# Cross-attention between tokens and states, then a feed-forward layer with the SERF activation: new orders for the first tenth of the program, and a one-element activation ahead of six activations that wait for two engines

## The chip, the core and the metric

The kernel runs on one core of a Trainium2 chip. The metric is the device time of one execution in microseconds (us). Five engines take part, each with a list of its own that it works through strictly in order: TensorE (PE; its weight loads are shown apart as PEld), VectorE (DVE), ScalarE (ACT), GpSimd (POOL) and SyncE (SP), which here only issues DMA transfers. An instruction that has to wait for another engine stops everything behind it in its own list. All products are in fp32.

## What is computed

```python
scores = scale * np.matmul(x, state.transpose(0, 1, 3, 2))     # x: 8 x 8 x 512 x 64, state: 8 x 8 x 32 x 64
a = softmax over the 32 states;      xread = np.matmul(a, state)
a2 = softmax over the 512 tokens of scale * state @ x^T;  sread = np.matmul(a2, x)
t = concatenate([xread, sread], axis=2)        # reshaped to 4352 x 512 (8 batches x 544 rows)

h = t @ w_in                                   # 512 x 2048
sp = np.maximum(h, 0.0) + np.log1p(np.exp(-np.abs(h)))        # softplus
g = h * erf(sp)
out = g @ w_out                                # 2048 x 512
```

## The kernel before

**Work.** The eight batches are handled one after the other, with 512 token rows each; the 32 state rows of all batches are gathered and handled together further back. The hidden width of 2048 is split into two halves u of 1024. For one batch and one half there is a *unit*: a first product into `h`, Softplus and Erf on ACT, the product with `h` on DVE, a second product with `w_out`. The units after batch 0 use a scheme that needs seven block products instead of eight; that is why DVE forms many sums and differences of blocks (`sums_y`, `sums_a`, `sums_w`, from lines 882, 996 and 1011).

**The first tenth.** Batch 0 and half u = 0 start with nothing loaded, and take another way (`begin0`, from line 382):

- `x` of batch 0 comes in four transfers of two heads each, two issued by ACT and two by SP. PE turns each part (L421), ACT or DVE copies it out of PSUM (`xT`, L164 or L170), and PE forms the scores (L447) in two groups g of four heads.
- For each group: copies of the scores, PE turns them (L453), DVE takes the maximum and subtracts it (L472, L474), ACT takes Exp (L477), DVE sums, inverts and multiplies (L479, L120 and L121, L482), PE turns the result (L457), and a copy makes `aT` (`ta0`, `ta1`).
- Meanwhile `w_in` and `w_out` of the first half arrive in pieces of 1 MB, in three buffers `raw`, and are rewritten by ACT and DVE (`convert`, from line 555: two activations L561 and L563, a shift L565, a sign step L570 or L573, an addition L579) because of a change of number format on the way.
- PE makes `m`, the product of `w_in` and the states (`mixed0`, L608), in parts: hidden blocks 0, 1, and 2 with 3. `first0` (L626) multiplies `m` with `aT`; ACT takes Softplus (L633) and Erf (L638); DVE multiplies (L642); `second0` (L651) multiplies with `w_out`, 32 products of 0.86 us. The first `first0` is the first product that isn't preparation.
- PE also turns the states of all batches (`turn_states`, L674), which come in two halves, `load_states` 0 and 1, four small transfers each (L662).
- Between these, PE runs spare products on the identity matrix (`spare_products`, L115), whose results nobody reads.
- The other direction of batch 0's attention (`later`, from line 490) takes its Exp on ACT (L498), and batch 1's attention (`attend`, from line 697) begins.

**What sets the order.** The kernel records every operation with `op(engine, cost, at, go, reads, writes, table)` into a list. `ORDER` then holds, written out by hand for each engine, the order in which that engine issues its operations; the numbers count the operations of that engine in recording order. `emit` merges the five lists into one program by estimated times, which doesn't alter an engine's own order, and `in_order` ties each instruction to the one before it on its engine. `BY_VECTOR` names copies that DVE makes; those that aren't named there ACT makes.

**Tables of ACT.** Exp, Softplus and Erf each need their own table in ACT. When the function changes, the compiler puts an ACT_TABLE_LOAD directly ahead of the activation. `op` is told of it by `table`. In the built program, an activation that waits for one engine has its load ahead of the wait; for some that wait for two engines, the first of the two waits stands ahead of the load and the second behind it. The program has 53 table loads before.

Two places far behind the first tenth matter too: the Softplus at 224.15 us (`first_product` of a later batch, `soft` at L971), which waits for DVE and PE, and the Softplus at 306.43 us, which waits for DVE and ACT itself. Behind each of them ACT makes copies (L961 and L919 in the one, L1280 in the other) that PE waits for.

Of the kernel before, what the change touches and what calls it, by code (L numbers as in the profile page):

```python
# [17 lines left out]
def kernel(  # L18
# [17 lines left out]
    nc = tc.nc  # L36
# [103 lines left out]
    def op(engine, cost, at, go, reads=(), writes=(), table=None, land=0.0, pipe=0.0):  # L140
# [14 lines left out]
        x0 s00 ta1 i00 i1 o0 o1 i2 i3 o2 o3 z0 z1 m000 m010 m011 m020 m021 u0 u1 m120 m121 tw1 sn10  # L155
        sn11 o9 i11 o11 i13 o13 i14 i15 o15 sn20 sn21 sn40 sn41 sn50 sn51 sn61 sn71""".split())

    def either(name, cost, out, in_, at, reads, writes, by=None, run=None):
# [15 lines left out]
        else:  # L174
# [4 lines left out]
            0 5 1-2 8 3 6 4 15 9 7 13 10 17 12 22 18 16 19 23 20 11 24-25 21 14 26 28 27 29-32 34 33  # L179
            45 70 69 62 53 46 61 54 71 48 55 35 72 37 56 36 38 64 39-40 49 41 47 50 73 57 74 58 60  # L180
            59 76 75 43 42 66 44 77-78 52 51 79-80 82 81 83 63 84 86 85 93 89 88 65 67 90 68 87 102
            91-92 94 97 103 106 95 107 104 108 105 109 118 114-115 110 116 96 111 117 119 99 98
            112-113 122 130 123-124 132-133 125 131 134 137 120 135 121 136 140 139 138 141 126
# [32 lines left out]
            0-1 5 2-3 6 4 13 12 8 7 15 14 9 17 31 16 11 18 10 20 51 19 52 32-34 36 21-22 35 24 37 23  # L216
            26 25 38-39 41 28 27 40 42 30 29 44 43 47 46 45 49 56 50 48 53-54 60 58-59 62 61 55 63
            96 65 64 66 69 67 70 72 68 89 71 90 74 81-82 73 83 75 84 78 77 76 79-80 85-88 57 91 146
            92 97 93 137 94 136 98-100 148 103 95 104 138-141 150 102 143 147 151 144 152 105 149
            153 101 142 154 159 155 161 160 157 156 162 164 158 163 165-168 145 172-173 169 175 174  # L220
            170 110 178 106-107 171 179 111 184 188 108 112 190 109 189 191 180 192 197 181-182 199
            198 200 194 193 195 202 113 201 196 204 185 177 176 211 210 114 183 186 203 214 213 212
            215 205-207 224 117 116 187 226 208 115 227 209 216 225 220 228 217 121 218 120 233 122
            234-235 118-119 236 238 237 229 123 239 241 247 246 221 219 240 231 251 250 232 248 222
            230 124 249 260 242-245 262 223 261 253 252 254 129 126 125 256 263 266 264 269 127 271
            128 272 255 273 268 275 130 270 131 258 132-133 284 283 285 282 135 257 134 276 274 265
            267 277-278 287-288 297 259 279-280 299 290 281 300 293 298 289 291 286 301 306 308
            303-304 309 307 294 302 312 292 311 314 310 313 295 305 315-317 296 322 319 318 320 345
            323 321 325 324 347 330 348 346 326 349 331 350 327-328 354 333 356 351 332 357 353 355
            358-359 361 334 340 352 329 360 335 362-363 341 364 336 365-366 343 342 338 344 337 387  # L230
            372 339 367-368 373 375 374 370 376 382 388 371 369 389-390 383 377 385 393 392 378 391
            395 394 400 396-397 384 379 398 380 402 399 381 403-404 401 407 386 408 415 413 416
            405-406 414 409 418 410-411 420-421 419 412 424 422 427 429 425 423 430 433 431 434 428
            432 426 435-437 440 438 443 442 441 417 439 464 466 465 449 444 467 450 445 470 452 468
            451 446 473 475 447 453 448 471 469 476 474 472 478 477 480 459 479 454 481-482 455 460
            483 488 486 489 462 487 461 484 510 457 485 463 456 511-512 458 513 495 490 514 519 496
            518 491 497 521 492 498 493-494 522 499 520 515 524 517 516 523 526 500 525 527-528 501
            534-535 505 532 503 529 502 533 506 530 507 556 508 558 531 559 509 504 536 560 557 541
            537 542 562 565 544 538 566 539 564 563 567-568 571 543 569 561 570 540 545-546 578-580
            573 581 551 572 574 552 575 602 576 554 553 577 547 604 549 548 605 550 603 555 606 587  # L240
            582 611 588 590 613 610 591 589 583 609 585 608 614 607 584 617 586 619 615 618 597 612
            616 620-621 598 592 626 622 624 627 625 594 599-600 593 648 595 601 623 596 633 650 649
            651-652 634-635 657 654 628-629 655 636 659 630 658 631 660 653 637 656 661 643 663 662
            664 632 644 665-666 646 645 667-668 670 673 638 672 639 647 669 640-641 671 694 642 696
            679 695 674 697-698 680 675 703 700 681 705 676-677 682 678 706 702 699 704 709 707 711
            684 683 689 716 719 701 718 708 710 685 712 717 740 713 690 714-715 691-692 687 741-743
            693 744 686 725 749 688 726 746 720 751 745 750 721 728 722 752 727 723 753 755 729 748
            747 756 724 754 735 757-758 730 759-760 731 761 736 733 732 738 737 734 739 762-763 765
# [1480 lines left out]
```

## Time and profile before

| | |
|---|---|
| median of three runs | 696.99 us (696.93 to 697.43) |
| the profiled execution | 696.16 us |
| its span in the trace | 694.3 us |
| granted TensorE clock | 0.999 |
| PE busy | 686.8 us |
| DVE busy | 581.7 us |
| ACT busy | 480.1 us |
| POOL busy | 85.8 us |

The span goes from the first to the last instruction in the trace; the execution's own time holds 1.86 us more around it. Times in the trace count from the start of the span. "Busy" adds up the instructions of an engine; in a row of the timeline the first number is the start, the second how long the row's instructions took from the first start to the last end, and a bracket at the end tells how long the engine had been idle before, and which engine and instruction ended that. PE rows follow each other with an overlap, because matmuls are pipelined: the distance from start to start is what a row costs.

### The profile page before, as it was taken

To read this page: it belongs to the slowest core of one execution; us is meant where nothing else is said; L and a number is where in the kernel's file an instruction comes from. 1 tells how busy PE (TensorE), PEld (TensorE's weight loads), DVE (VectorE), ACT (ScalarE), POOL (GpSimd) and SP (SyncE) were. 2 spreads that over 40 slices of the span, in tenths; PEclk is the share of its full clock that TensorE was granted. 3 is DMA by queue.
4 is the path that set the end of the run, shared out by engine and by line. 5 is a ranking of instruction groups with operands and counts; after the bars stand their busy time and mean duration, and the time that the engine had idled before them with its cause. 6 is when DMAs were issued, how large, how long until landed. Compare 5 with 4: busy or idle time off the path is not lost.

```text
span 694.3 us, 13176 instructions
## 1 busy us (share of the span) xinstructions
PE 686.8 (99%) x5193; PEld 584.0 (84%) x5193; DVE 581.7 (84%) x899; ACT 480.1 (69%) x850; POOL 85.8 (12%) x93
## 2 busy tenths in 40 slices
PE   9999999999999999999999999999999999999997
PEld 8435678787878788889998879898989898989997
DVE  5999899998989799989945779785969586949897
ACT  6987998988886695747255574848574857477742
POOL 0001000010001110000100000024101331312312
PEclk9999999999999999999999999999999999999999
DMA  9847976977889517425454302436322663721675
GB/s 266 231 141 177 180 233 155 216 199 187 287 171 276 169 49 267 125 84 152 119 157 166 84 1 61 122 42 119 46 69 31 118 89 71 105 31 18 89 138 107
DMA packets 133741, 92.87 MB, mean 134 GB/s; under 512 B 93744, under 2 KB 120752, under 8 KB 133168
## 3 DMA queue, kind: packets, MB, share of 16 engines
q1 hardware_dynamic: 113648, 61.29, 32.3%
q0 software_dynamic: 18800, 29.63, 22.8%
q10 hardware_dynamic: 1232, 1.11, 0.5%
q8 instruction: 41, 0.67, 0.4%
q14 instruction: 20, 0.16, 0.1%
HBM read 50.86 MB, written 41.16 MB: 133 GB/s over the span
## 4 chain that ended last, share of the span: by engine, by line
PE 93%; DVE 4%; ACT 1%; DMA 1%; issue 1%; SPq 0%; DVEq 0%; ACTq 0%
PE o L1270 31%; PE h L949 18%; PE o L1033 16%; PE at L949 7%; PE o L651 4%; PE o L1454 4%; PE h L1405 3%; PE h L850 2%; PE at L850 2%; PE at L626 1%; PE at L1405 1%; DVE ring L1000 1%; PE at L811 1%; PE h L718 1%; DMA x<-in_x_dram 1%; PE o L115 1%
## 5 line engine op out<-in xcount | busy, mean ns | idle before, releaser
L961 ACT COPY ring<-h 128x512 f32<-128x512 f32 x120 | 69.4, 586 | 70.9 <-PE h L949 66.3
L989 DVE TENSOR_TENSOR ring<-ring 128x1024 f32<-128x1024 f32 (+1 forms) x64 | 72.9, 1151 | 24.9 <-ACT ring L986 24.3
L949 PE MATMUL h<-aT,m 128*128 128x256 f32 x360 | 92.0, 380 | 0.0
L971 ACT ACTIVATE ring<-ring 128x512 f32<-128x512 f32 x120 | 72.2, 631 | 10.8 <-DVE ring L967 4.9
L1033 PE MATMUL o<-w_out,ring 128*128 128x256 f32 x320 | 77.1, 381 | 0.0
L1000 DVE TENSOR_TENSOR ring<-ring 128x1024 f32<-128x1024 f32 x60 | 72.6, 1217 | 0.4
L949 PEld LDWEIGHTS h<-aT,m 128*128 128x128 f32 x360 | 65.3, 190 | 8.5 <-issue 1.0
L1033 PEld LDWEIGHTS o<-w_out,ring 128*128 128x128 f32 x320 | 59.9, 190 | 13.1 <-issue 2.5
L1270 PE MATMUL o<-w_out,w_in 128*128 128x128 f32 x512 | 68.7, 275 | 0.0
L1270 PEld LDWEIGHTS o<-w_out,w_in 128*128 128x128 f32 x512 | 64.3, 192 | 1.5
L1270 PE MATMUL o<-w_out,ring 128*128 128x128 f32 x480 | 64.7, 275 | 0.6 <-ACT oo L1280 0.6
L1270 PEld LDWEIGHTS o<-w_out,ring 128*128 128x128 f32 x480 | 60.6, 192 | 3.0 <-ACT oo L1280 1.0
L986 ACT ACTIVATE ring<-ring 128x1024 f32<-128x1024 f32 (+1 forms) x64 | 62.8, 1007 | 0.2
L1033 PE MATMUL o<-raw,ring 128*128 128x256 f32 x240 | 58.9, 380 | 0.0
L1033 PEld LDWEIGHTS o<-raw,ring 128*128 128x128 f32 x240 | 45.1, 190 | 7.1 <-issue 0.8
L1270 PE MATMUL o<-raw,ring 128*128 128x128 f32 x360 | 49.5, 275 | 0.0
L1270 PEld LDWEIGHTS o<-raw,ring 128*128 128x128 f32 x360 | 46.1, 192 | 2.0 <-DVE sc L1285 0.8
L1270 PEld LDWEIGHTS o<-raw,xT 128*128 128x128 f32 x320 | 38.8, 192 | 3.7 <-ACT o L1301 2.5
L1270 PE MATMUL o<-raw,xT 128*128 128x128 f32 x320 | 41.5, 277 | 0.0
L1189 POOL DMA_DIRECT2D out_dram<-oo x16 | 23.0, 1526 | 126.0 <-ACT x L1280 62.3
L949 PE MATMUL h<-sy,sx 128*128 128x256 f32 x120 | 31.4, 385 | 0.8 <-ACT h L919 0.8
L949 PE MATMUL h<-sy,m 128*128 128x256 f32 x120 | 31.1, 382 | 0.0
(269 smaller groups left out, 1398.8 us busy)
## 6 DMA issues: line engine op xcount, KB each, us to landing
x<-in_x_dram SPq DMA_DIRECT2D x30, 256.0 KB, 5.0
xq<-in_x_dram SPq DMA_DIRECT2D x112, 64.0 KB, 2.6
out_dram<-oo SPq DMA_DIRECT2D x10, 512.0 KB, 3.9
raw<-in_moe_w_in_dram SPq DMA_DIRECT2D x8, 512.0 KB, 6.5
raw<-in_moe_w_out_dram SPq DMA_DIRECT2D x4, 1024.0 KB, 6.2
raw<-in_moe_w_in_dram POOLq DMA_DIRECT2D x8, 512.0 KB, 6.5
raw<-in_moe_w_out_dram POOLq DMA_DIRECT2D x8, 512.0 KB, 5.5
kept_a<-aT SPq DMA_DIRECT2D x8, 512.0 KB, 4.5
```

The source lines that it names most:

```text
L651: nc.tensor.matmul(out=bank("o%d" % r), lhsT=gT[g][:, i, P * r:P * r + P], rhs=w_out[:, GF * g + i, :], start=(made_of[r] == 1), stop=(mad ...
L850: nc.tensor.matmul(out=bank(names[k])[Ns * p:Ns * p + Ns, :], lhsT=st[r, b, q], rhs=of_group[2 * u + j][r, :, i, :], start=True, stop=True)
L949: nc.tensor.matmul(out=out_[:, i], lhsT=x_[:, q:q + P], rhs=y_, start=(start and i == 0), stop=(i == 1), skip_group_check=not start)
L961: op(ACT, 0.5, t, lambda: nc.scalar.copy(out_(), view(bank(name))), [name], w)
L971: op(ACT, 0.53, t, lambda: nc.scalar.activation(out=part(splane, k), in_=part(hplane, k), func=ACTF.Softplus), area(hplane, ks=[k], os=[o] ...
L986: op(ACT, 0.085 + 0.875 * share, at + n, lambda s_=s_: nc.scalar.activation(out=s_, in_=s_, func=ACTF.Erf), [], area(splane, ks=[k], os=os ...
L989: op(DVE, 0.065 + 1.075 * share, at + n + 1, lambda s_=s_, h_=h_: tt(s_, s_, h_, op=ALU.mult), area(hplane, ks=[k], os=os), area(splane, k ...
L1000: op(DVE, 1.14, at + k, lambda k=k, x_=x_, y_=y_, how=how: tt(get("h", k), get(*x_), get(*y_), op=how), area(v[x_[0]], ks=[x_[1]]) + area( ...
L1033: nc.tensor.matmul(out=view(name)[:, h], lhsT=lhs[:, i, :], rhs=weight_of[n]()[:, u, i, :], start=(start and h == 0 and i == 0), stop=(h = ...
L1270: nc.tensor.matmul(out=out_[:, Q2 * k:Q2 * k + Q2], lhsT=lhs[:, k, i], rhs=rhs[:, i], start=first, stop=(k == len(ns) - 1 and i == 1), ski ...
L1405: nc.tensor.matmul(out=bank(bk)[:, P * i:P * i + P], lhsT=x_[:, i, k], rhs=y_[:, k], start=(start and i == 0 and k == 0), stop=(i == GF - ...
L1454: nc.tensor.matmul(out=bank("o%d" % bk)[:, E2 * c:E2 * c + E2], lhsT=ring[:, w_[w], plane, k][:, i, :], rhs=weight_of[n]()[:, u, i, :], st ...
```

## The change

Two things are changed in the code.

**1. The first tenth.** `ORDER` is rewritten for the first 79 of 821 operations on PE, 62 of 786 on ACT (64 of 788 after), 90 of 889 on DVE (88 of 887), 25 of 98 on SP and 5 of 84 on POOL; behind that, the order is the same as before on each engine (all numbers on ACT grow by two and those on DVE fall by two, because two more copies are recorded for ACT). `BY_VECTOR` moves these copies:

- from DVE to ACT: the scores `s00`, `aT` half `ta1`, a sign step `i00`, `m000` and `m011`, the copy `tw1`, the state copy `z1`;
- from ACT to DVE: `x3`, the scores `s11`, the sign step `i01`, and `m100` and `m101`.

In the new order the second group of heads goes first: its two parts of `x` are loaded, turned and scored ahead of the first group's, and its half of the first `w_in` piece is loaded and converted ahead of the other half. SP issues the first half of the state loads ahead of the first load for batch 1, and the second 1 MB of `w_out` ahead of the second half of the state loads and of the first loads `xq` for batch 1; further loads `xq` change places with pieces of `w_in` and `w_out`. On ACT the two Exp of the other direction of batch 0 (L498) move from ahead of the first Softplus to between two pairs of Softplus and Erf; on DVE the sums for batch 0 (`sums_y`) move ahead, and on PE the `second0` products change places among each other. On POOL one staged `w_in` load moves ahead, and one staged `w_out` load behind, the store of a piece of batch 0's output.

**2. The one-element activation.** While it goes through the operations, `emit` counts the table loads on ACT; ahead of the operations at loads 2, 4, 9, 11, 26 and 33 it issues an activation of the same function on one element per partition. It reads a constant and writes a tile `spark` that nothing reads. The table load then stands ahead of this activation, and neither waits for another engine. The program has 54 table loads after. Loads 2, 4 and 9 are those of a Softplus of `first0`, load 11 that of Exp in batch 1's attention (L753 before), and loads 26 and 33 are those of the Softplus at 224.15 us and at 306.43 us in the profile before.

```diff
     BY_VECTOR = set("""
-        x0 s00 ta1 i00 i1 o0 o1 i2 i3 o2 o3 z0 z1 m000 m010 m011 m020 m021 u0 u1 m120 m121 tw1 sn10
-        sn11 o9 i11 o11 i13 o13 i14 i15 o15 sn20 sn21 sn40 sn41 sn50 sn51 sn61 sn71""".split())
+        x0 x3 s11 i01 i1 o0 o1 i2 i3 o2 o3 z0 m010 m020 m021 u0 u1 m100 m101 m120 m121 sn10 sn11 o9
+        i11 o11 i13 o13 i14 i15 o15 sn20 sn21 sn40 sn41 sn50 sn51 sn61 sn71""".split())
...
         PE: """
-            0 5 1-2 8 3 6 4 15 9 7 13 10 17 12 22 18 16 19 23 20 11 24-25 21 14 26 28 27 29-32 34 33
-            45 70 69 62 53 46 61 54 71 48 55 35 72 37 56 36 38 64 39-40 49 41 47 50 73 57 74 58 60
-            59 76 75 43 42 66 44 77-78 52 51 79-80 82 81 83 63 84 86 85 93 89 88 65 67 90 68 87 102
+            0 5 3 15 4 1-2 7-8 6 12 17-18 9 13 22 19-21 16 23 25 10-11 24 14 26 28 27 30 29 32 31
+            33-34 46 70 54 53 45 61-62 69 47 56 64 35 72 55 37 36 38 48 71 40 39 41 58 57 50 74 73
+            49 59-60 42-43 75 52 51 44 77-78 76 79 66 82 81 80 83 63 84 86 85 93 89 88 65 67 90 68
...
         ACT: """
-            0-1 5 2-3 6 4 13 12 8 7 15 14 9 17 31 16 11 18 10 20 51 19 52 32-34 36 21-22 35 24 37 23
-            26 25 38-39 41 28 27 40 42 30 29 44 43 47 46 45 49 56 50 48 53-54 60 58-59 62 61 55 63
+            1 0 4 3 2 7 15-16 5-6 12-14 8 10 33 32 17-19 9 34 20 11 35 21 36-37 22 38-39 24 40 23 26
+            25 52 28 27 53 42 41 30 43 29 44-45 47-48 46 50-51 58 49 54 31 55 57 56 61 64 63 62 60
...
         DVE: """
-            0-1 72 2 13-14 73 3 16 15 7 4 8 5 41 6 17 9-10 74 11 42-43 18 12 19-20 22 44-45 21 23 49
-            48 58 47 79 75 24 46 25 28 26 50-51 27 29-30 77 59 80 31 61 32 76 60 34 53 52 82 33 35
-            55 54 117 36-38 65 62 57 66 56 63 40 64 118 81 78 67-70 87-88 83-84 89 85 71 90 86 103
+            1 0 2 72 15 8 16 9 3 13 4 14 71 17 5 10 6 40 7 11-12 18-20 22 77 73 78 42 41 21 43 23 80
+            46 44-45 24-26 28 58 57 47-48 27 29-31 50 49 60 34 32 74 33 76 35 52 51 59 37 75 53-54
+            36 79 115 38 64 61 65 55-56 62-63 116 66-69 85-87 81-82 70 83 88 84 101 89 102 90
...
         SP: """
-            1 0 2 5-6 8 7 9 17 3-4 18 10 23 12 11 13 24 19 14 21 20 15 22 16 25-26 28 27 31 34 29-30
+            1-2 0 6 5 7-9 3 10 4 18 17 11 20 12 14 19 13 15 24 23 16 21-22 25-26 28 27 31 34 29-30
...
         GP: """
-            1 4 6-7 0 5 2 9-10 12-13 8 16 15 11 18 3 14 19 24 17 20-22 25 27 23 26 28-29 31 30 32-34
+            1 4 7 0 6 5 2 9-10 12-13 8 16 15 11 18 3 14 19 24 17 20-22 25 27 23 26 28-29 31 30 32-34
...
     }
+    EARLY = {2, 4, 9, 11, 26, 33}
+    spark = const.tile([P, 1], F32, name="spark")
+
+    def ahead(n):
+        func = {"softplus": ACTF.Softplus, "erf": ACTF.Erf, "exp": ACTF.Exp}[ops[n][5]]
+        go = ops[n][3]
+
+        def after():
+            nc.scalar.activation(out=spark, in_=nc.const_aps.tensor(1.0, [P, 1], F32), func=func)
+            go()
+
+        ops[n] = (*ops[n][:3], after, *ops[n][4:])
+
...
         order = sorted(begin, key=lambda n: (begin[n], n))
+        loaded, loads = None, 0
+        for n in order:
+            table = ops[n][5]
+            if ops[n][0] == ACT and table not in (None, loaded):
+                loaded, loads = table, loads + 1
+                if loads in EARLY:
+                    ahead(n)
         for n in order:
             ops[n][3]()
```

More of the change, by code (lines that the diff above doesn't have):

```diff
@@ L221 @@
[L221 to L240, printed above, removed]
@@ new lines @@
+            374 341 369-370 375 377 376 372 378 384 390 373 371 391-392 385 379 387 395 394 380 393
+            397 396 402 398-399 386 381 400 382 404 401 383 405-406 403 409 388 410 417 415 418
+            407-408 416 411 420 412-413 422-423 421 414 426 424 429 431 427 425 432 435 433 436 430
+            434 428 437-439 442 440 445 444 443 419 441 466 468 467 451 446 469 452 447 472 454 470
+            453 448 475 477 449 455 450 473 471 478 476 474 480 479 482 461 481 456 483-484 457 462
```

115 lines of the change are left out of this document (65 added, 50 removed).

## The prediction

> **What bounds the kernel now.** I read the busy shares and the chain first.
>
> ```profile
> PE 686.8 (99%) x5193; PEld 584.0 (84%) x5193; DVE 581.7 (84%) x899; ACT 480.1 (69%) x850; POOL 85.8 (12%) x93
> PE 93%; DVE 4%; ACT 1%; DMA 1%; issue 1%; SPq 0%; DVEq 0%; ACTq 0%
> ```
>
> PE is busy all the time and carries the chain. So there are only two ways to gain: let PE's real work begin earlier (the spare products in front count as busy, but end nothing), or close the few places where it stands still. The timeline of PE, read to the end for its brackets, has three of these from 60 us on, at 225.91, at 307.65 and a small one further back. The first two are where the change puts its last two small activations. The timeline of all engines around the first, and behind it a row of DVE and the small halt of PE:
>
> ```profile
> 218.12 0.58 ACT L961 COPY ring<-h 128x512 f32<-128x512 f32 x1
> 222.10 0.68 DVE L963 TENSOR_TENSOR ring<-ring,at 128x512 f32<-128x512 f32 x1
> 222.86 1.28 ACT L971 ACT_TABLE_LOAD   x1 [4.16 <-DVE ring L963]
> 223.18 1.89 PE L1033 MATMUL o<-raw,ring 128*128 128x256 f32 x8
> 224.15 0.63 ACT L971 ACTIVATE ring<-ring 128x512 f32<-128x512 f32 x1
> 224.69 0.57 ACT L961 COPY ring<-h 128x512 f32<-128x512 f32 x1
> 225.29 0.57 ACT L919 COPY h<-h 128x512 f32<-128x512 f32 x1
> 225.91 1.13 PE L949 MATMUL h<-sy,sx 128*128 128x256 f32 x4 [0.84 <-ACT h L919]
> 226.88 1.03 PE L949 MATMUL at<-aT,sx 128*128 128x256 f32 x4
> ...
> 232.33 0.69 DVE L963 TENSOR_TENSOR ring<-ring,at 128x512 f32<-128x512 f32 x1 [1.52 <-PE at L949]
> ...
> 539.79 0.71 PE L1270 MATMUL o<-raw,w_in 128*128 128x128 f32 x4 [0.19 <-ACT ot L1280]
> ```
>
> ACT is idle for 4.16 us, then DVE's sum at L963 ends, and only now the table is loaded, 1.28 us; Softplus and two copies follow without a gap, and PE waits for the second. Around the second place:
>
> ```profile
> 302.71 2.35 DVE L1000 TENSOR_TENSOR ring<-ring 128x1024 f32<-128x1024 f32 x2
> 304.01 0.27 ACT L1280 COPY ot<-o 128x128 f32<-128x128 f32 x1
> 305.14 1.28 ACT L971 ACT_TABLE_LOAD   x1 [0.85 <-DVE ring L1000]
> 305.98 1.03 PE L949 MATMUL at<-aT,sx 128*128 128x256 f32 x4
> 306.43 0.63 ACT L971 ACTIVATE ring<-ring 128x512 f32<-128x512 f32 x1
> 307.65 1.61 PE L1270 MATMUL o<-w_out,ring 128*128 128x128 f32 x12 [0.64 <-ACT oo L1280]
> 309.09 1.03 PE L949 MATMUL h<-sy,sx 128*128 128x256 f32 x4
> ```
>
> The same picture with less idle time ahead. For the first tenth, a stretch of busy times (PE, PEld, DVE, ACT and POOL in this order), the timeline of PE, PEld, DVE, ACT and SP, and the transfers by group (the last number is the median from issue to landing):
>
> ```profile
> 30.00:70.00 40.00, 40.00 (x237) 17.82 (x236) 39.29 (x53) 33.02 (x44) 3.36 (x5) 1.00 0.66 168
> 18.11 0.56 ACT L170 COPY aT<-o 128x512 f32<-128x512 f32 x1
> 20.32 1.16 ACT L561 ACTIVATE w_out<-raw 128x1024 f32<-128x1024 f32 x1
> 9.67 0.69 DVE L472 TENSOR_REDUCE m1b<-at 128x16 f32<-128x512 f32 x1 [0.36 <-PE at L453]
> 16.76 0.69 DVE L579 CUSTOM_DVE_ANT_0 w_in<-raw,w_in 128x1024 uint16<-128x1024 uint16 x1 [0.34 <-ACT raw L573]
> 18.58 0.69 DVE L482 TENSOR_TENSOR ring<-ring,z1b 128x512 f32<-128x512 f32 x1
> 19.47 0.60 PE L457 MATMUL o<-ident,ring 128*128 128x128 f32 x4
> 19.91 3.60 PE L626 MATMUL h<-aT,m 128*128 128x512 f32 x8
> 20.19 0.68 DVE L164 COPY aT<-o 128x512 f32<-128x512 f32 x1
> 22.04 1.23 DVE L579 CUSTOM_DVE_ANT_0 w_in<-raw,w_in 128x2048 uint16<-128x2048 uint16 x1
> 23.44 0.66 PE L608 MATMUL at<-w_in,ring 64*32 64x256 f32 x16
> 24.31 0.76 DVE L164 COPY m<-at 128x256 f32<-128x256 f32 x2
> 25.12 0.30 PEld L626 LDWEIGHTS at<-aT,m 128*128 128x128 f32 x2 [0.35 <-DVE m L164]
> 29.26 0.41 DVE L887 TENSOR_TENSOR sy<-aT 128x256 f32<-128x256 f32 x1
> 15.41 3.48 SPq L662 DMA_DIRECT2D st<-in_state_dram  x4
> 20.04 1.29 SPq L587 DMA_DIRECT2D raw<-in_moe_w_out_dram  x1
> raw<-in_moe_w_out_dram SPq DMA_DIRECT2D x4, 1024.0 KB, 6.2
> ```
>
> DVE hardly rests (39.29 of 40 us, and two idle times of a third of a us in the rows before that), so its list decides when PE's real work begins: the second multiply (18.58) ends, PE turns its result (19.47), and the first real product follows at 19.91. From 30 us on PE has no gap in the whole tenth (40.00 of 40.00 us).
>
> **The sum, part by part.**
>
> *The load at 222.86.* With the small activation, load and activation are free to run from 218.70 (218.12 + 0.58). The activation itself isn't in the trace. A Softplus on 512 elements takes 0.63 us and a copy of 128 elements 0.27 us, so I bound one element between 0.1 and 0.3 us and take 0.2. Both end at about 220.2, long before DVE. Softplus starts at 222.86 instead of 224.15, and the copies end 1.29 us earlier; PE could go on at 224.62. Is PE ready then? In a full stream a group starts 0.17 us before the row ahead ends (223.18 + 1.89 = 225.07, so at 224.90). PE would therefore not wait: it gains 225.91 − 224.90 = 1.0, and the first group after the halt, which costs 0.97 (225.91 to 226.88) instead of 0.86, another 0.1. I take **1.1 us**; the bounds are the idle time of 0.84 and the 1.29 by which ACT is earlier.
>
> *The load at 305.14.* It can start at 304.28 (304.01 + 0.27), 0.86 us earlier, but the small activation's 0.2, less some overlap, goes in between: Softplus at about 305.72 instead of 306.43, 0.7 us earlier. DVE's L1000 ends at 305.06 and doesn't delay it. PE could use more: by 0.17 before 307.01 it would be ready at 306.84, 0.81 before 307.65, so ACT stays last there and the gain is **0.7 us** (bounds 0.5 and 0.9).
>
> *What moves behind these places.* After the first, DVE waits for PE again at 232.33, so it has 1.52 us to spare and follows; and from the second on PE is dense, so both gains stay. Nothing else in the unchanged part gets an instruction.
>
> *The added load and the other four small activations.* Two Exp now stand between a Softplus-Erf pair and the next, which adds one load of 1.28 us; four small ones are 0.8 us; the copies that change engine give ACT about 0.5 us net and take as much from DVE. That is 2.6 us more on ACT, which has 40.00 − 33.02 = 7.0 us free between 30 and 70 us. I cost it at nothing. Without that cover each microsecond would reach PE through Softplus and DVE's product.
>
> *When the real products begin.* Up to the second multiply the two DVE lists hold nearly the same instructions: the sign step, the score copy and the `m` copy of the one half for those of the other. The idle times of 0.36 and 0.34 us go; a new one of some 0.6 us comes ahead of the first shift, since its ACT step waits for the first half of `w_in` and that lands no earlier than now. So the multiply, and with it PE's turn, comes by my count of the two lists 0.2 to 0.5 us earlier. On ACT the copy that the first product needs (0.56 us) now stands behind a conversion of the first `w_out` (1.16 us), which waits for a 1 MB transfer; this takes back part. I take **0.3 us**, between −0.5 (the transfer lands late) and +0.7.
>
> *From there to 25.12.* Before, DVE does the two copies of `m`, a copy of `aT` (20.19, 0.68 us) and the shift, sign and addition (ending 23.27) before PE's `mixed0` at 23.44; then comes another sign step, up to 24.31, and the copies of `m` (to 25.07), and PE's weight load waits for these, 0.35 us. After, the `aT` copy and an earlier `m` copy are ACT's, some 0.9 us less on DVE; two sums (0.41 each) come in between, but behind the addition, and DVE starts this stretch some 0.6 us earlier, since its multiply is earlier and one `m` copy stands ahead of it. DVE's copies of `m` then end near 24.3. PE, from 19.6 with four halves of `first0` (3.53, from 19.91 to 23.44) and `mixed0` and the states (1.35, from 23.44 to 25.12 less the wait), gets to its next `first0` at 24.5 and need not wait: **0.3 us**.
>
> *From 25.12 to the common order.* PE is dense before, so other places of its products can gain nothing, and each new wait is a loss. ACT now makes one conversion step (1.16 us) before the Softplus of the second pair, whose Erf and DVE product come close to PE's need; I take **−0.2 us** (bounds 0 and −1).
>
> *The queues.* SP's second half of the states (15.41) and two `xq` loads go behind the second 1 MB of `w_out`, which is issued as soon as its buffer is free. The addition at 16.76 reads that buffer last; the new DVE list has it ahead of two steps more, at about 15.5. By 6.2 us from issue to landing it lands at about 22, and the states, small, behind it at 22.5 to 23.5. PE turns them at about 23.6. I cost this at nothing, with little to spare: the states being late by a microsecond would stop PE for one. The later swaps bring `w_in` and `w_out` pieces no later than now. POOL's three swapped transfers feed conversions that come after 90 us in an unchanged order: nothing.
>
> Sum: 1.1 + 0.7 + 0.3 + 0.3 − 0.2 = 2.2 us. The profiled execution has 696.16 us, so 693.96 after it; the median of the runs, 696.99, is 0.83 higher, which gives 694.8 us.
>
> **A rule against it.** In the trace a load costs ACT its own 1.28 us and no more:
>
> ```profile
> 23.50 1.08 ACT L633 ACTIVATE ring<-h 128x512 f32<-128x512 f32 x2
> 24.61 1.28 ACT L638 ACT_TABLE_LOAD   x1
> 25.90 1.06 ACT L638 ACTIVATE ring<-ring 128x1024 f32<-128x1024 f32 x1
> ```
>
> From load to activation are 1.29 us, and the load starts 0.03 us after the activations ahead of it have ended (23.50 + 1.08). The Trainium skill (ScalarE: Activation LUTs, What ACT_TABLE_LOAD costs) counts a drain of 1380 ns beside the load's 1283 ns, 2.66 us for every switch, and advises to do everything of one table set before changing; by that the second place would lose and the added switch in the first tenth weigh double. The load's length agrees with the trace, the drain doesn't show.
>
> **Rivals.**
>
> *Only the late loads pay.* The first tenth comes out even or slightly worse, because DVE's list is as full as before and the gain at 19.91 goes to the `w_out` conversion or to the second pair's Softplus: 1.8 us less a few tenths, 695.2 to 695.8. For it: each of the three early terms is of the size of my error in it.
>
> *Switches cost more where they follow work.* If a switch cost a second load's length, 1.28 us, as a halt behind it, load and small activation from 304.28 would end near 307.0, later than 306.43: a loss of 0.6. The added switch and halt would eat more of ACT's free time, and I count half a load, 0.6, as a loss; the first place still gains 1.1 and the early part 0.4: 697.0 − 1.1 + 0.6 − 0.4 + 0.6 = 696.7, no change. The rows from 23.50 on speak against it. The rule of the Trainium skill (ScalarE: Activation LUTs) would, with its 1380 ns, make this 0.1 us more per switch.
>
> *The states come late (slower).* If the 1 MB lands only 10 us after its issue, or the small transfers take their turn well after it, PE stands ahead of `turn_states` with everything behind. The loss is the landing time of the states minus 23.6. It eats the forecast from 25.8 on, and makes the kernel slower by 0.2% from 27.2 on; at 28 it would be 699.2. For it: the 6.2 us is a median of four and says nothing of the longest, and SP took 3.48 us to issue these small transfers. Against: it would have to be late by 2.2 us before the forecast is eaten.
>
> *The first tenth gains more.* DVE's list is shorter by about 1.3 us up to the common order. If PE follows it, 693.5.
>
> **How the numbers follow.** The forecast has 0.46, only the late loads 0.22, dearer switches 0.07, late states 0.10, the greater gain 0.15. About 0.2%, 1.4 us, is what a measurement of this kernel can tell from no change. The forecast and the greater gain are faster, and of the second case two thirds (up to 695.6): 0.46 + 0.15 + 0.15 = 0.76. The same: the rest of the second case and the switches, 0.14. Slower: 0.10. The range goes from 693.2 (the greater gain with the upper bounds of the late places) to 696.3, which takes in the second case with a wait of 0.5 more, and leaves out the late states, most of the switches and a little beyond.
>
> **What will show it.** Right: both late table loads inside ACT's idle time, so that Softplus follows DVE at once, and no bracket on PE there, or one of 0.1 us at the second; the first `first0` before 19.8 us; no bracket on PE between 25 and 70. Wrong: PE waiting ahead of the turned states, or for DVE's product of the second pair; a load followed by more than 1.29 us; or a new halt behind 226 us that gives the gain back.

## The result, and the profile after

The changed kernel takes 694.36 us (median of six executions, 693.91 to 695.24), the kernel before, beside it on the same chip, 697.12. The ratio is 0.9964, with a 95% interval of 0.9953 to 0.9976: 1.7 to 3.3 us faster. The forecast was 694.8. The profiled execution has 693.91 us and a span of 691.8 us, against 696.16 and 694.3 before; the granted clock is 1.00 in both.

The page's busy shares and its chain:

```profile
PE 686.5 (99%) x5193; PEld 585.0 (85%) x5193; DVE 581.2 (84%) x897; ACT 483.0 (70%) x859; POOL 85.8 (12%) x93
PE 99%; DVE 0%; DVEq 0%; issue 0%
```

The chain now is PE's alone; before, 4% of it were DVE's and 1% ACT's. Line numbers have grown by 20 behind the inserted code, so Softplus of a later batch is L991 and the small activation L308. The timeline around the first late place, and PE's row behind it:

```profile
217.94 0.58 ACT L981 COPY ring<-h 128x512 f32<-128x512 f32 x1
...
218.54 1.28 ACT L308 ACT_TABLE_LOAD   x1
219.84 0.20 ACT L308 ACTIVATE spark<-const-float32-1.0 128x1 f32<-128x1 f32 x1
...
221.85 0.68 DVE L983 TENSOR_TENSOR ring<-ring,at 128x512 f32<-128x512 f32 x1
222.62 0.63 ACT L991 ACTIVATE ring<-ring 128x512 f32<-128x512 f32 x1 [2.58 <-DVE ring L983]
222.90 1.89 PE L1053 MATMUL o<-raw,ring 128*128 128x256 f32 x8
...
223.76 0.57 ACT L939 COPY h<-h 128x512 f32<-128x512 f32 x1
...
224.63 1.03 PE L969 MATMUL h<-sy,sx 128*128 128x256 f32 x4
225.50 1.03 PE L969 MATMUL at<-aT,sx 128*128 128x256 f32 x4
```

The load follows the copy at once, the small activation ends at 220.04, and ACT then idles for 2.58 us; Softplus starts when DVE's sum is there. PE has no bracket. The product at 226.88 before stands at 225.50: 1.38 us earlier, of which 0.28 were there already at 222.90 (223.18 before). This place gained 1.10 us. The second place:

```profile
302.63 0.27 ACT L1300 COPY ot<-o 128x128 f32<-128x128 f32 x1
302.92 1.28 ACT L308 ACT_TABLE_LOAD   x1
...
304.21 0.20 ACT L308 ACTIVATE spark<-const-float32-1.0 128x1 f32<-128x1 f32 x1
304.32 0.61 ACT L991 ACTIVATE ring<-ring 128x512 f32<-128x512 f32 x1
...
305.52 1.60 PE L1290 MATMUL o<-w_out,ring 128*128 128x128 f32 x12
...
306.96 1.03 PE L969 MATMUL h<-sy,sx 128*128 128x256 f32 x4
```

309.09 has become 306.96, 2.13 us earlier, so this place gave 0.75. Here the load fills ACT's idle time and Softplus follows the small activation without a gap. In the program the difference looks like this (second place, before and after):

```
LoadActFuncSet                        [waits DVE]
Activation ring<-ring 128x2x256       [waits Activation]

LoadActFuncSet
Activation spark<-const 128x1
Activation ring<-ring 128x2x256       [waits DVE, Activation]
```

The first tenth, by PE's timeline and the busy times of the stretch that the prediction looked at (PE, PEld, DVE, ACT, POOL):

```profile
6.68 1.47 PE L441 MATMUL o<-ident,x 128*128 128x128 f32 x12
...
20.16 2.84 PE L646 MATMUL h<-aT,m 128*128 128x512 f32 x6
...
25.25 3.60 PE L646 MATMUL at<-aT,m 128*128 128x512 f32 x8
28.69 9.71 PE L671 MATMUL o<-w_out,ring 128*128 128x512 f32 x22
...
71.03 1.02 PE L671 MATMUL o<-w_out,ring 128*128 128x512 f32 x2
```

```profile
30.00:70.00 40.00, 40.00 (x238) 18.25 (x237) 39.50 (x56) 36.88 (x54) 3.37 (x5) 1.00 0.70 174
```

The first real product starts at 20.16, 0.25 us later than before, and still the common order is reached 0.28 us earlier (71.03 for 71.31). Between 30 and 70 us ACT has 36.88 us of work instead of 33.02 and no bracket stands on PE. Behind 309 us another 0.35 us are gained that the prediction doesn't have: 0.14 near 479 us and 0.21 at 540, where the wait of 0.19 is gone. 0.28 + 1.10 + 0.75 + 0.35 = 2.48, which is the difference of the spans within 0.01 us.

### The profile page after: what moved, and what is told of

Its sections match the earlier page's. It is cut to its first block, busy times and chain, and to the rows that moved or that the text cites. A ratio compares the mean times of both kernels' runs of the same rounds, so it can differ in the third digit from the quotient of the medians.

```text
span 691.8 us, 13184 instructions
## 1 busy us (share of the span) xinstructions
PE 686.5 (99%) x5193; PEld 585.0 (85%) x5193; DVE 581.2 (84%) x897; ACT 483.0 (70%) x859; POOL 85.8 (12%) x93
## 3 DMA queue, kind: packets, MB, share of 16 engines
q10 hardware_dynamic: 1232, 1.11, 0.5%
## 4 chain that ended last, share of the span: by engine, by line
PE 99%; DVE 0%; DVEq 0%; issue 0%
PE o L1290 32%; PE h L969 19%; PE o L1053 18%; PE at L969 8%; PE o L671 4%; PE o L1474 4%; PE h L1425 3%; PE h L870 2%; PE at L870 2%; PE o L115 2%; PE h L646 1%; PE at L831 1%; PE at L1425 1%; PE at L646 1%; PE h L738 1%; PE o L441 0%
## 5 line engine op out<-in xcount | busy, mean ns | idle before, releaser
L991 ACT ACTIVATE ring<-ring 128x512 f32<-128x512 f32 x120 | 72.2, 632 | 13.9 <-DVE ring L987 4.9
```

What stands on the lines that cost most here:

```text
L991: op(ACT, 0.53, t, lambda: nc.scalar.activation(out=part(splane, k), in_=part(hplane, k), func=ACTF.Softplus), area(hplane, ks=[k], os=[o] ...
```

## The experiments

### The late places alone, and the orders alone

```diff
 # late_only: kernel before, its own ORDER and BY_VECTOR, with emit's counting and ahead()
+    EARLY = {25, 32}
 # orders_only: changed kernel
-    EARLY = {2, 4, 9, 11, 26, 33}
+    EARLY = set()
```

> The kernel before, with its own orders, and a one-element activation ahead of two Softplus only: those whose loads stand at 222.86 and 305.14 us. Theory (the late places pay by themselves): PE has no idle time left at either, 1.10 and 0.75 us are gained there, as in the changed kernel, and nothing in the first tenth: 1.85 us in the trace, about 695.3 us against 697.1. Rival (the new first tenth is needed for it, since ACT or PE stands differently there): less than half of it, 696.3 us or more. Further back, at 479 and at 540 us, PE became another 0.1 and 0.2 us earlier in the changed kernel, in code that is the same: if that comes from being earlier at these places it shows here too (695.0), if from something in the first tenth it doesn't.

> The changed kernel without any of the six small activations: the new orders of the first tenth alone. Theory (the two parts add up): the gain of 0.28 us that the trace shows for the first tenth stays, and 1.85 us of the late places are lost again: about 696.6 us, 0.3 to 0.8 below before. The two late loads stand behind their waits again and PE waits for ACT at both, 0.84 and 0.64 us. Rival (the four early small activations are what pays in the first tenth): no gain in the first tenth, or a loss, 697.1 us or more.

The late places alone: 694.84 us against 696.55, ratio 0.9977 (0.9968 to 0.9986), 1.0 to 2.2 us faster. By the trace they gain 1.11 and 0.74 us. The orders alone: 695.93, ratio 0.9991 (0.9982 to 1.0), 0 to 1.25 us faster; both late waits are back (0.86 and 0.64 us) and nothing is gained there. So the two parts add up within their intervals (1.7 and 0.6 us by the medians, 2.8 together in the changed kernel), and each late place depends on its own small activation and on nothing in the first tenth. Of the 0.35 us behind 309 us, the 0.21 at 540 is missing with the late places alone and there with the orders alone, so it comes with the orders; both gain 0.15 near 479, but had lost 0.16 near 397. The profile of the late places alone also has a row that the first profile of before doesn't have:

```profile
46.62 3.70 PE L646 MATMUL at<-aT,m 128*128 128x512 f32 x8 [0.57 <-DVE m L164]
538.61 0.71 PE L1290 MATMUL o<-raw,w_in 128*128 128x128 f32 x4 [0.19 <-ACT ot L1300]
```

In this execution the old orders lose 0.6 us in the first tenth, and the wait at 540 is there. The profile of the orders alone has neither. Both are taken up below.

### A second load

```diff
                 if loads in EARLY:
                     ahead(n)
+                if loads in (26, 33):
+                    ahead(n, "erf" if loads == 26 else "exp")
```

> The changed kernel with one more table load and small activation at each of the two late places, of another function, ahead of the one that is there: 1.28 + 0.20 = 1.48 us more on ACT at each. Theory (a load costs its own 1.28 us, and only what is longer than ACT's idle time reaches PE): at the first place 2 x 1.48 = 2.97 us fit into the 3.9 us from 218.7 to 222.62 and nothing is lost; at the second Softplus starts at 305.9 instead of 304.32 and PE loses 1.3 to 1.6 us: 695.8 us. Rival (each load brings a drain of 1.38 us beside its 1.28): 2 x 2.86 = 5.7 us at the first place, 1.8 us more than there is, and at the second 2.8 us or more: together some 4.5 us, 698.9 us.

695.47 us, ratio to before 0.9983 (0.9975 to 0.9992). ACT at the first and at the second place, and PE at the second:

```profile
218.74 1.28 ACT L308 ACT_TABLE_LOAD   x1
220.03 0.20 ACT L308 ACTIVATE spark<-const-float32-1.0 128x1 f32<-128x1 f32 x1
220.25 1.28 ACT L308 ACT_TABLE_LOAD   x1
221.55 0.20 ACT L308 ACTIVATE spark<-const-float32-1.0 128x1 f32<-128x1 f32 x1
222.95 0.63 ACT L993 ACTIVATE ring<-ring 128x512 f32<-128x512 f32 x1 [1.20 <-DVE ring L985]
...
304.77 1.28 ACT L308 ACT_TABLE_LOAD   x1
306.06 0.20 ACT L308 ACTIVATE spark<-const-float32-1.0 128x1 f32<-128x1 f32 x1
306.17 0.61 ACT L993 ACTIVATE ring<-ring 128x512 f32<-128x512 f32 x1
```

```profile
307.37 1.60 PE L1292 MATMUL o<-w_out,ring 128*128 128x128 f32 x12 [1.41 <-ACT oo L1302]
```

At the first place 1.20 us are left over behind two loads, and nothing is lost. At the second, PE waits 1.41 us; by its products the place goes from a gain of 0.75 to a loss of 0.77 against before, 1.52 us. A load with its small activation costs 1.51 us from start to start (218.74 to 220.25), and only what outlasts ACT's idle time reaches PE. The drain of 1380 ns that the Trainium skill (ScalarE: Activation LUTs, What ACT_TABLE_LOAD costs) counts beside each load doesn't show here either: the load at 220.25 starts 0.02 us after an activation, and the one behind it 0.02 us after the load. The prediction's second rival falls.

### Does a conversion on ACT hold the first product?

```diff
         ACT: """
-            1 0 4 3 2 7 15-16 5-6 12-14 8 10 33 32 17-19 9 34 20 11 35 21 36-37 22 38-39 24 40 23 26
+            1 0 4 3 2 7 15-16 5-6 12-14 8 10 33 32 17-18 9 34 19 11 20 35 21 36-37 22 38-39 24 40 23 26
```

> The changed kernel with two copies of aT moved on ACT: each ahead of the activation on the first w_out piece that it stood behind (1.18 and 1.23 us). Theory (the first real product is late because its copy waits for that activation, not for PE's turn): the copy starts at about 19.2 instead of 19.50, and PE's first real product at 19.85 instead of 20.16; the wait for the second copy goes too. Of these 0.3 to 0.5 us PE keeps 0 to 0.4 at the common order, since the w_out activations and the Softplus behind come 0.6 us later: 694.0 to 694.4 us. Rival (DVE's multiply and PE's turn are what is late): the first product stays at 20.1 and the time is that of the changed kernel or up to 0.5 us longer.

694.45 us, ratio 0.9966 (0.9953 to 0.9978), as the changed kernel. Its timeline:

```profile
17.99 0.69 DVE L502 TENSOR_TENSOR ring<-ring,z1b 128x512 f32<-128x512 f32 x1
18.37 0.83 PE L115 MATMUL o<-ident 128*128 128x128 f32 x6
18.57 0.58 ACT L170 COPY aT<-o 128x512 f32<-128x512 f32 x1 [0.61 <-PE o L477]
19.04 0.60 PE L477 MATMUL o<-ident,ring 128*128 128x128 f32 x4
19.48 2.74 PE L646 MATMUL h<-aT,m 128*128 128x512 f32 x6
27.86 0.69 DVE L662 TENSOR_TENSOR ring<-ring,h 128x512 f32<-128x512 f32 x1 [0.54 <-ACT ring L658]
28.60 1.98 PE L671 MATMUL o<-w_out,ring 128*128 128x512 f32 x4 [0.19 <-DVE ring L662]
```

19.48 looks like the expected gain, but this execution began 0.6 us earlier too (PE's turns of x at 6.06, not 6.68). From those turns the distance is 13.42 us, against 13.48: 0.06 us. The copy does go earlier, but in PE's list the second turn, at 19.04, stands ahead of the product, and counted from the turns of x it hasn't moved. DVE's multiply isn't what it waits for: that ends at 18.68, and before, the turn came 0.20 us behind it (19.27 and 19.47). Here PE is busy with six spare products until 19.04, 0.36 us behind the multiply. The price is as expected: w_out's conversions and Softplus come later, DVE waits 0.54 us for Erf, and PE for DVE. My step that put the lateness on the conversion was wrong.

### The start, again and again

The next two have no edit: the changed kernel and the kernel before once more.

> The changed kernel once more, for the spread of its start. In the executions so far PE's first turn of x began between 4.70 and 5.42 us, whatever the kernel. Theory (in the new orders one chain, without slack, leads from there to the first real product): the first real product is 14.75 +- 0.05 us behind that turn, so anywhere between 19.45 and 20.2, and what lies 0.6 us later at the start stays later to the end. Rival (the first product is set by a transfer of w_in or w_out, with its own time): the distance changes by some tenths while the first product stays where it was, at 20.16. By the theory the span is 691.2 to 691.8 us.

> The kernel before once more, for what differs between executions of one and the same program. Theory (the first tenth of the old orders has waits for transfers that come and go): the first real product stays within 0.1 us of 19.9, wherever the first turn of x begins (4.70 with 19.91 in the first profile, 5.25 with 19.84 in the run with the old orders), PE's product at 71.31 us moves by some tenths, and the waits at 225.91 (0.84), 307.65 (0.64) and 539.79 us (0.19) are there again. Rival: the first product follows the first turn here too (20.4 if the turn is at 5.2); and the wait of 0.19 us comes and goes.

693.95 us (ratio 0.9965, 0.9952 to 0.9977) with a span of 691.4, and one execution of 697.02. Times in us of PE's first turn of x, of the last turns of x ahead of the scores (the third group of four with the old orders, the group of twelve with the new), of its first real product and of the common product (71.31 in the first profile):

| profile | first turn | last turns | first product | common product | between the two |
|---|---|---|---|---|---|
| old orders, first | 4.70 | 6.70 | 19.91 | 71.31 | 51.40 |
| old, late places | 5.25 | 6.63 | 19.84 | 71.94 | 52.10 |
| old, again | 5.52 | 7.25 | 20.45 | 72.23 | 51.78 |
| new orders, first | 5.37 | 6.68 | 20.16 | 71.03 | 50.87 |
| new, again | 5.00 | 6.31 | 19.79 | 70.58 | 50.79 |
| new, no early ones (below) | 4.99 | 6.30 | 19.78 | 70.96 | 51.18 |
| new, orders alone | 4.78 | 6.09 | 19.56 | 70.33 | 50.77 |
| new, second load | 5.42 | 6.73 | 20.19 | 71.11 | 50.92 |
| new, banks (below) | 5.52 | 7.11 | 20.57 | 71.64 | 51.07 |

In the new orders the first product is 13.46 to 13.48 us behind the last turns, in all six: one chain without slack, as expected. With the old orders it is 13.20 or 13.21 us behind theirs, in all three, so it follows the start there too, and that part of my expectation fell. (From the very first turn the distance isn't constant, 14.77 to 15.05 us in the new orders; the last turns are the better mark.)

The start varies by a microsecond between executions of what is the same program up to there. It isn't the arrival of x: only in the first profile of before does a turn in this table wait for x (0.41 us at 5.76). What varies is how long PE's first products run at half of their later pace. Rows of the changed kernel's first profile:

```profile
0.78 3.75 PE L115 MATMUL o<-const-float32-1.0 128*128 128x128 f32 x16 [0.78 <-PEq L1733]
12.27 3.29 PE L115 MATMUL o<-ident 128*128 128x128 f32 x28
```

From start to start of the next row (4.46 and 15.49), the sixteen products take 0.23 us each and the twenty-eight 0.115. By the starts of the single products in the traces the full pace comes at 3.6 us in the first profile of before and at 6.3 in the second, at 5.1 and 4.2 in the two of the changed kernel. The profile's clock column has 1.00 in these stretches, so it doesn't show this; what sets the moment, no run shows.

On the mean the first product comes at 20.07 with the old orders and at 20.01 with the new. Profiles that start alike tell it better. With the first turn at 5.52 the old orders have it at 20.45 and the new at 20.57, both in the banks profile and in that of the states with half the delay (below). DVE's second multiply starts at 19.12 in the old orders there, and at 19.03 and 19.02 in the new, so DVE's list got 0.1 us shorter; but PE's turn of the result goes from 20.01 to 20.09 and 20.07, behind the spare products. So nothing is gained at the first product; that the spare products are the reason is read from the rows, and no run leaves them out.

The gain lies behind it. From the first product to the common one the old orders take 51.76 us, the new 50.93, 0.8 us less. Part of it shows in the second execution of the old orders, in PE's timeline:

```profile
46.88 3.70 PE L626 MATMUL at<-aT,m 128*128 128x512 f32 x8 [0.28 <-DVE m L164]
```

and back along the late-places profile, 0.57 us at 46.62, in the timeline of ACT and DVE, with the rows of SP that issue the last piece of this part of `w_in`, there and in the changed kernel:

```profile
36.64 1.18 ACT L583 ACTIVATE raw<-raw 128x1024 uint32<-128x1024 uint32 x1 [0.77 <-DVE ring L662]
38.88 0.69 DVE L585 TENSOR_SCALAR w_in<-w_in 128x1024 uint32<-128x1024 uint32 x1 [0.86 <-ACT w_in L581]
...
30.19 1.54 SPq L564 DMA_DIRECT2D raw<-in_moe_w_in_dram  x1
...
28.88 0.49 SPq L564 DMA_DIRECT2D raw<-in_moe_w_in_dram  x1
```

ACT's conversions of w_in are held up, DVE's shift waits for them, and PE for DVE's copies of m behind it. In the first profile of before none of the three waits is there; in the second they are 0.47, 0.58 and 0.28 us. No profile with the new orders has a wait at that place.

What holds ACT is the landing of that piece, for which this conversion waits in the built program. (The bracket names DVE's product, but that had ended at 36.16.) In the late-places profile it lands 6.4 us after the start of its issue, at 36.6, and the conversion starts at 36.64; in the second profile of before it lands at 36.86 (31.86 and 5.0), and the conversion starts at 36.91. In the first profile it lands at 35.69, just before ACT comes to it at 35.84. The old orders issue it behind four loads `xq`, at 30.2 to 31.9 us; the new orders behind two of them, at 28.3 to 29.3, and in all six it lands 0.5 to 1.0 us before ACT comes to it. So the new order on SP takes away a wait that comes and goes with the transfers. The two profiles with the wait are 0.4 and 0.7 us longer between the two products than the one without; no run changes this order on SP alone.

### The four early small activations

```diff
-    EARLY = {2, 4, 9, 11, 26, 33}
+    EARLY = {26, 33}
```

> The changed kernel with the small activations at the two late places alone, and not at the four places of the first tenth (Softplus of the first product, Exp of batch 1's attention). Theory (ACT's idle time hides where a load stands in the first tenth): PE's product at 71.03 us in the changed kernel comes 65.6 to 65.8 us after the first turn of x, against 65.66 there, and the time is that of the changed kernel within 0.3 us. Rival (the early ones carry the gain of the first tenth): the distance grows by 0.3 us or more and a wait of PE for DVE's product or for ACT appears between 25 and 60 us.

693.54 us (ratio 0.9959, 0.9946 to 0.9971), 0.4 below the changed kernel beside it, which five executions each can't tell from nothing. The profile has a longer distance, 65.97 from the first turn (4.99) to the common product, and so by the letter speaks for the rival; but the wait that makes it is of a transfer:

```profile
33.56 1.30 DVE L729 STREAM_TRANSPOSE xq<-xq 128x512 f32<-128x512 f32 x2 [0.37 <-DMA xq<-in_x_dram]
35.49 2.84 PE L671 MATMUL o<-w_out,ring 128*128 128x512 f32 x6 [0.16 <-DVE ring L662]
```

Up to 28.30 it is within 0.01 us of the changed kernel's second profile on PE, and the second Softplus is even 0.17 us earlier (29.64 for 29.81). The run with the orders alone lacks the early ones too and has the shortest distance of all (65.55). They gain nothing and cost nothing that can be seen.

### The states made late

```diff
         SP: """
-            1-2 0 6 5 7-9 3 10 4 18 17 11 20 12
+            1-2 0 6 5 7-9 3 10 18 17 4 11 20 12        # states_late, states_late2
+            1-2 0 6 5 7-9 3 10 18 4 17 11 20 12        # states_half
```

> The changed kernel with the second half of the state loads behind four transfers of xq on SP, so about 4.1 us later (20.5 instead of 16.42). This is the slower rival of the prediction made true: PE turns the states at 24.49 in the changed kernel and waits there for what isn't landed. Theory (the loss is the landing minus 24.4): the last one is issued at about 22.0 and lands 5.6 us later, at 27.6; PE stands for 3.1 us, and the whole comes to 697.4 us, no faster than before. Rival (there is slack behind, or the transfers land sooner when they are later, since less is under way): a halt under 1.5 us, 695.9 us or less.

> The kernel with the states' second half behind four transfers of xq once more. The first profile of it was the slowest of nine executions: PE waited 1.98 us for the states at 27.20, and then ran at a granted clock of 0.56 for some four us, which cost another 1.7 us; the median of the nine is 1.3 us above the changed kernel. Theory (the length of the halt varies with the transfers, and a short one leaves the clock alone): here the halt is 0.5 to 1.5 us, the clock stays at 1.00 behind it, and the loss is the halt alone, 694.6 to 695.6 us. Rival (the clock falls after any halt at this place): half clock again, 2 us or more lost in all.

> The changed kernel with the states' second half behind two transfers of xq instead of none, so about 1 to 2 us later. Theory (the states had 0.5 to 1 us to spare): PE waits 0 to 1 us ahead of the turned states, the granted clock stays at 1.00, 694.0 to 695.2 us. Rival (no slack): a halt of 1.5 us or more, with the clock falling behind it, 696 us or more.

The median of nine executions is 695.22 us, ratio 0.9976 (0.9966 to 0.9987), 1.3 above the changed kernel on the same chip. They spread from 694.16 to 698.24, and the profiled one is the slowest. PE in it, and the stretches behind (the third figure from the end is the granted clock):

```profile
27.20 1.71 PE L694 MATMUL o<-ident,st 128*128 128x128 f32 x7 [1.98 <-DMA st<-in_state_dram]
28.70 4.56 PE L646 MATMUL at<-aT,m 128*128 128x512 f32 x8
33.10 7.46 PE L671 MATMUL o<-w_out,ring 128*128 128x512 f32 x17
```

```profile
27.00:29.00 2.00, 1.80 (x8) 1.83 (x9) 0.06 (x1) 1.99 (x3) 0.00 (x0) 0.56 1.16 234
29.00:31.00 2.00, 2.00 (x4) 0.72 (x4) 2.00 (x3) 1.78 (x3) 0.00 (x0) 0.59 0.97 211
31.00:33.00 2.00, 2.00 (x6) 0.91 (x5) 2.00 (x5) 0.60 (x1) 0.00 (x0) 1.00 0.49 118
```

The halt is 1.98 us, and then PE runs at half clock, for 3.4 us (in stretches of 0.2 us the clock is 0.50 from about 27.2 to 30.6): the turned states take 1.50 us instead of 0.76 (27.20 to 28.70), the eight products 4.40 instead of 3.44, another 1.7 us. With the same program once more, 695.58 us:

```profile
26.19 0.95 PE L694 MATMUL o<-ident,st 128*128 128x128 f32 x7 [1.65 <-DMA st<-in_state_dram]
26.98 3.60 PE L646 MATMUL at<-aT,m 128*128 128x512 f32 x8
```

The halt is 1.65 us, a little over the expected range, and the rows behind have their full speed: the loss is the halt. With half the delay, 694.00 us, no wait at all. SP had ended the issue of the states at 18.35 in the changed kernel; 20.04 costs nothing and 23.42 costs 1.65 us. The transfers are quicker when later, 5.6 us from issue to landing in the median of the four in the changed kernel, 3.2 and 3.1 in the two late ones, so the halt stayed well under the expected 3.1 us. The median speaks for the rival; the one execution beyond the expected 697.4 got there by the half clock, which neither had.

### The wait at 540 us

```diff
+        for b in ("o0", "o1", "o2", "o3"):
+            bank(b)
         for n in order:
             ops[n][3]()
```

> The changed kernel with its four o accumulators in PSUM made in the order in which the kernel before makes them (o0 o1 o2 o3; the new order of PE makes them o0 o2 o3 o1). At 539.79 us the kernel before has a wait of PE for ACT of 0.19 us, behind an addition by DVE that starts 0.2 us later than its inputs; all four runs with the new orders don't have it, and the run with the old orders and the late small activations has it. Theory (it hangs on which bank an accumulator lies in): the wait of 0.19 us is back near 537.5 us. Rival (it comes from the times at which the engines arrive there): no wait there.

694.93 us in one execution, and no wait there. The wait of 0.19 us is in all three profiles with the old orders and in none with the new, though DVE's and PE's lists at that place are the same instruction by instruction. In the old orders DVE's addition starts 0.21 us after the end of ACT's copy, in the new at its end. It isn't the order of the banks. What it is stays open.

## Why the prediction was right, and where it wasn't

*The bound, and the load at 222.86.* Forecast 1.1, measured 1.10, 1.11 with the old orders, and nothing without the small activation. The step held as put: load and small activation end at 220.04 (forecast 220.2), the cover is DVE's, and PE doesn't wait. *The load at 305.14.* Forecast 0.7, measured 0.75 and 0.74. The small activation, which no row of before showed, takes the 0.20 us assumed; it was right to count it here, where the cover of 0.86 us is too short for it.

*When the real products begin.* Forecast 0.3 earlier; measured 0.25 later in the profile, 0.06 earlier in the mean over three and six executions, 0.12 later where the start is alike. This step failed. It took DVE's list for what decides, but DVE's multiply came only 0.1 us earlier where 0.2 to 0.5 were counted, and behind it PE's own list, with its spare products, holds the turn. The delay that it subtracted, the conversion ahead of ACT's copy, isn't one either (0.06 us with the copy moved). And one execution's start was taken as given, while it varies by a microsecond with PE's pace in its first products.

*From there to 25.12, and from 25.12 to the common order.* Forecast 0.3 and −0.2, together 0.1; in the profile 0.53, in the mean 0.8. The first of them came out at 0.13 (20.16 to 25.25, against 19.91 to 25.13): PE doesn't wait at 25.25. The second had the wrong sign. The new wait that I priced at 0.2, Softplus of the second pair, didn't come, and I overlooked two things in the profile of before. A PE without gaps in a busy-time row isn't a PE at its pace: the 22 products took 9.78 us there (28.66 to 38.44) and 9.64 after (28.69 to 38.33). And the old lists sat close to a wait for DVE's copies of m at 46 us, because a piece of w_in landed only 0.15 us ahead of ACT; one profile without brackets doesn't show this, and two of three executions have the wait. The medians differ by 2.76 us and the two profiles by 2.25, which fits this. The rival that the first tenth gains more was right in this term, though not by DVE's shorter list alone.

*The queues.* Costed at nothing: for the states rightly, and the slack was larger than I put it, as 1.7 us of delay cost nothing. For the later swaps it was wrong: "no later than now" was true, but earlier was worth something, since the piece of w_in that now goes ahead of two loads `xq` is the one that ACT had to wait for. And the price of the slower rival was too low in one respect: the landing minus 23.6 is the loss only while the halt is short.

*The added load and early activations.* Costed at nothing: rightly, with less cover than stated. ACT's work between 30 and 70 us grew by 3.9, not 2.6 us, and 3.1 us are left. *Behind 306 us* the forecast has nothing, and 0.35 us came: 0.21 of it with the new orders, unexplained, and 0.14 near 479, open too.

So the sum, 2.2 us, holds because its two large terms were measured places with a named cover. Of the three terms of the first tenth, together 0.4 forecast and 0.3 in the profile, 0.9 in the mean, one has the wrong cause and one the wrong sign: that their sum comes near is luck.

## What to carry to other kernels

An activation that waits for two engines can hold its table load behind the first of the waits; where ACT idles ahead of it and PE waits behind it, one activation on one element per partition moves the load into the idle time and costs 0.2 us. Its worth can be read in one row: the load's 1.28 us, less what doesn't fit into the idle time, and not much more than the wait of PE that it ends (here 1.10 and 0.75 us gained where the brackets had 0.84 and 0.64). For orders in the first microseconds one profile of each kernel isn't enough: compare distances from a row that starts the chain, over several executions, or profiles that start alike. And where a bracket names an instruction that had long ended, look for a transfer that landed just then.

## What was unexpected of the hardware

A halt of PE can cost more than its length: behind 1.98 us of waiting the granted clock was 0.50 for 3.4 us and added 1.7 us; behind 1.65 us, in another execution of the same program, it stayed at 1.00. The Trainium skill (TensorE: Matmul & The Clock Gate, Part 1) says that the array falls to half its clock after about an idle window of 3.4 us, and that the windows run freely. The half clock agrees, and it lasted as long as the page's window; the halt that brought it was shorter than that window here. Whether the length of the two halts or their moment made the difference, no run shows.

Small halts have a price too. The eight products behind the wait of 0.35 us before took 3.53 us from start to start (25.13 to 28.66), the eight that followed without a wait after 3.44 (25.25 to 28.69): 0.09 us for the restart, as in the 0.97 instead of 0.86 us behind the halt at 225.91.
